# Reciprocals' transfers moved from SyncE to POOL, and weight pieces decoded three steps after their load

## The chip, the cores and the metric

The kernel runs on one core of one Trainium2 chip. Its engines are TensorE (PE, with its weight loads PEld), VectorE (DVE), ScalarE (ACT), GpSimd (POOL) and SyncE (SP), which here issues nearly all transfers. The metric is device time in microseconds (us), as a median of runs. Single rows come from one profiled execution.

## The reference, cut to what matters

Softcapped attention without a mask, a gated block that mixes over the sequence, and a block with a gated convolution, all in float32, one after the other.

```python
def _attn_ref(q, k, v, cap):                  # (2, 12, 448, 64)
    scores = scale * np.matmul(q, k.transpose(0, 1, 3, 2))
    scores = cap * np.tanh(scores / cap)
    scores = scores - np.max(scores, axis=-1, keepdims=True)
    attn = np.exp(scores)
    attn = attn / (np.sum(attn, axis=-1, keepdims=True) + 1e-09)
    return np.matmul(attn, v)

def _moe_ref(x, w_in, g_ln, w_sg, b_sg, w_out):   # x (2, 448, 768), w_in (768, 1024)
    h = gelu(x @ w_in)
    u, v = h[..., :512], h[..., 512:]
    v_n = layernorm(v) * g_ln
    v_s = np.einsum('ts,bsd->btd', w_sg, v_n) + b_sg[None, :, None]
    return x + (u * v_s) @ w_out

def _moe2_ref(x, w_in, conv_w, w_out):
    h = relu(x @ w_in)
    return (h * sigmoid(conv3(h, conv_w))) @ w_out
```

## The kernel before, in words

Every float32 product is made of three matmuls on numbers split into a high and a low part. The weights come from memory as 64-bit numbers and are decoded on the chip: `decode` loads a piece of 128 x 512 (512 KB, line 123) into a buffer named `f64` and turns it in three steps into the two parts. Step one is `L128` (ScalarE) and `L133` (VectorE), step two `L138`, `L141` and the cast `L147`, step three the subtraction `L150` (VectorE). `wait` says how many ticks after the load each step is issued, `bufs` how many pieces may be held at once.

Attention runs over 12 passes N, one pair of heads each, in two halves; a half is one round R, with two ticks in it (`tick()`), and `later(k, fn)` puts work k ticks ahead. In a half TensorE makes the scores `sc` (keys by queries), ScalarE takes tanh (`L312`) and exp (`L313`) of them into `raw`, and one round later, from round 13 on two rounds later, TensorE multiplies by the values (`pv`) and adds up the rows (`su`). VectorE sums two parts of `raw` beforehand (`sm`, `L333`), splits the keys and queries of a later pass (`L90`, `L93`, `L258`, `L259`) and copies the row sums out of `su` (`se<-su`, `L380`). There is one buffer for `su`, so the next pass's `su` waits for that copy, and one for `sc`, so the next scores wait for the tanh. In some rounds TensorE also starts the input product of the next block (`mo`, "fill").

The first ten passes are normalised in twos. I call such two passes a couple; there are five. When the second pass of a couple is summed, `norm` sends the sums from 4 to 128 partitions (`ss<-se`, line 385). Three ticks later `s1` adds a guard and takes the reciprocal (`L393`, `L394`) and writes it to memory (`d<-ss`, 397). `s1b` reads it back four times, spread over the partitions (`rb<-d`, 403), and `s2` multiplies (`E<-E,rb`, `L410`) and splits the result into `X`, the input of the next block (`L92` on ScalarE, `L93` on VectorE). The last two passes are normalised by TensorE.

```python
            later(3, s1)
            later(5, s1b)
            later(10, s2)
```

Each engine works in order. The order itself comes from a scheduler that issues instructions when its own model finds them ready, so ticks give the order of the program text and the scheduler may move an instruction within it. Line 442 is where pieces of `w_in` are asked for, in the rounds that `WIN` gives: 0, 3, 6, 8, 10, 12, 12, 16, 17, 19, 20 and 20.

Of the kernel before, what the change touches and what calls it, by code (L numbers as in the profile page):

```python
# [20 lines left out]
NK = DM // P  # L21
# [25 lines left out]
def stages(  # L47
# [17 lines left out]
    nc = tc.nc  # L65
    V, A, T, G = nc.vector, nc.scalar, nc.tensor, nc.gpsimd
# [4 lines left out]
    def pin(last):  # L71
        return tc.issue_after(last[0].ins) if last[0] is not None else ExitStack()
# [3 lines left out]
    def later(k, fn):  # L76
        due.setdefault(now[0] + k, []).append(fn)
# [7 lines left out]
    def f(ap):  # L85
        return ap.bitcast(F32)

    def split(raw, hi, lo, hi_eng="v"):
        if hi_eng == "v":
            V.tensor_copy(hi, raw)  # L90
        else:
            A.activation(hi, raw, AF.Copy)  # L92
        return V.tensor_tensor(out=lo, in0=raw, in1=f(hi), op=ALU.subtract)  # L93
# [17 lines left out]
    cw = const.tile([P, 2, 3 * NF], F32R, name="cw")  # L111
# [7 lines left out]
    def decode(hi, lo, src, pool, bufs, wait=(1, 2, 3), hi_eng="a", cols=512, low_eng="v"):  # L119

        n = src.shape[1]
        r = pool.tile([P, cols, 2], U32, tag="f64", name="f64", bufs=bufs)[:, :n]
        nc.sync.dma_start(r, src)
        h, l = r[:, :, 1], r[:, :, 0]

        def s1():
            with pin(lasta), pin(lastv):
                A.activation(f(h), f(h), AF.Copy, scale=2.0**-112)  # L128
                if low_eng == "a":

                    A.activation(l, l, AF.Copy, scale=0.93 * 2.0**-29)  # L131
                else:
                    V.tensor_scalar(  # L133
                        out=l, in0=l, scalar1=29, scalar2=None, op0=ALU.logical_shift_right
                    )

        def s2():
            V.scalar_tensor_tensor(  # L138
                out=l, in0=h, scalar=3, in1=l, op0=ALU.logical_shift_left, op1=ALU.bitwise_or
            )  # L140
            V.scalar_tensor_tensor(  # L141
                out=l, in0=h, scalar=0x80000000, in1=l, op0=ALU.bitwise_and, op1=ALU.bitwise_or
            )
            if hi_eng == "a":
                A.activation(hi, f(l), AF.Copy)
            else:
                V.tensor_copy(hi, f(l))  # L147

        def s3():
            V.tensor_tensor(out=lo, in0=f(l), in1=f(hi), op=ALU.subtract)  # L150

        for k, fn in zip(wait, (s1, s2, s3)):
            later(k, fn)

    def wdec(dst, src, k, c0, c1, pool, bufs, **kw):
        c = slice(c0 % dst.shape[3], c0 % dst.shape[3] + c1 - c0)
        decode(dst[:, 0, k, c], dst[:, 1, k, c], src[k * P : (k + 1) * P, c0:c1], pool, bufs, **kw)

    def wi_piece(src, h, k):
        return WI[h], src, k, h * DH, (h + 1) * DH  # L160
# [51 lines left out]

    def columns(pool):
        nc.sync.dma_start(gbc, g_ln.partition_broadcast(P))
        decode(cw[:, 0], cw[:, 1], conv_w, pool, 3)

    def attention(att, psa):

# [45 lines left out]
        def prep_k(n):  # L264
            _, kr = qraw.pop(n)
            K = Kt[n % 2]
            lastv[0] = split(kr, K[:, 0], K[:, 1], "a" if n == 0 else "v")
# [67 lines left out]
        def values(N, half):  # L335
# [28 lines left out]
            if half:  # L364
                del acc[N]
                norm(N, ps, su)

        def norm(N, ps, su):
            b, p = divmod(N, NPAIR)
            if N >= B * NPAIR - NFAST:  # L370
                return norm_pe(N, ps, su)

            j = N % 2
            if j == 0:
                pairs[:] = (
                    att.tile([P, 2, S // 2], F32, tag="se", name="se", bufs=2),
                    att.tile([P, 2, S], F32, tag="E", name="E", bufs=3),
                )
            se, e = pairs
            V.tensor_copy(se[:, j], su)  # L380
            A.activation(e[:, j], ps, AF.Copy)
            if j == 0:
                return
            ss = att.tile([P, 14], F32, tag="ss", name="ss", bufs=2)
            nc.sync.dma_start(ss, se[::32])
            rb = att.tile([P, 2, S], F32, tag="rb", name="rb", bufs=2)

            ds = []


            def s1():
                with pin(lastv):
                    V.tensor_scalar(out=ss, in0=ss, scalar1=guard, scalar2=None, op0=ALU.add)  # L393
                V.reciprocal(out=ss, in_=ss)  # L394
                ds.append(dr.tile([2, 2, 2, S // 2], F32, tag="d", name="d"))
                d = ds[0]
                nc.sync.dma_start(d.rearrange("h f j (p c) -> (h f j p) c", c=14), ss)

            def s1b():
                (d,) = ds  # L400
                for h in range(2):
                    for i in range(2):
                        nc.sync.dma_start(  # L403
                            rb[h * D : (h + 1) * D, i].rearrange("p (f c) -> p f c", f=2),
                            d[h, :, i].partition_broadcast(D),
                        )

            def s2():
                with pin(lastv):
                    V.tensor_tensor(out=e, in0=e, in1=rb, op=ALU.mult)  # L410
                with pin(lasta):
                    lastv[0] = split(e, X[:, 0, p - 1 : p + 1, b], X[:, 1, p - 1 : p + 1, b], "a")

            later(3, s1)
            later(5, s1b)
            later(10, s2)

        def norm_pe(N, ps, su):

# [19 lines left out]
        for R in range(2 * NN + LAGS[1]):  # L439
            N, half = divmod(R, 2)  # L440
            if R == 1:
                columns(att)
            for j, at in enumerate(WIN):
                if int(at * 4 + 1) // 2 == R:
                    wdec(*wi_piece(w_in, j // NK, j % NK), att, 3, hi_eng="v")
            if R < 2 * NN:
                if half == 0 and N + 2 < NN:
                    load(N + 2)
                scores(N, half)
                if half == 0 and N + 1 < NN:  # L450
                    prep_q(N + 1)
                    prep_k(N + 1)
            if R in FILL:

                i, k0, k1 = FILL[R]
                if k0 == 0:
                    fill[i] = psm.tile([P, 512], F32, tag="mo", name="mo")[:, :S]
                for k in range(k0, k1):
                    mmw(fill[i], 0, i, k, ordered)
                if k1 == NK:  # L460
                    u_done(0, i, fill[i])
            tick()
            if R - done >= LAGS[R >= LAGS[2]]:
                values(*divmod(done, 2))
                done += 1
            if half and N + 1 < NN:
                load_v(N + 1)
            tick()
# [411 lines left out]
```

## Time and profile before

| | |
|---|---|
| Time, median of 3 runs | 354.4 us (354.24 to 354.47) |
| Profiled execution: its time, its span | 356.76 us, 354.9 us |
| TensorE matmul, weight loads: busy | 333.1 us (94%), 252.5 us (71%) |
| VectorE, ScalarE, POOL: busy | 253.2 us (71%), 225.4 us (64%), 14.1 us (4%) |
| Mean granted clock of TensorE | 0.965 |
| Chain that ended last, by engine | PE 76%, DMA 10%, DVE 7%, SP's queue 3%, ACT 2% |

The span is the time from the first to the last instruction. Busy is the time in which the engine has an instruction in work; transfers are issued on a queue, which doesn't count as busy. Attention ends at about 141 us. POOL works in the first 5 us and then not before 141 us.

### The profile page before, as it was taken

The page shows a single profiled execution, that of the slowest core. Times are in us where ns is not written, and L with a number is a line of the kernel's source. Part 1 is how long each engine was busy: PE and PEld are TensorE (multiplying, and loading weights), DVE is VectorE, ACT ScalarE, POOL GpSimd, SP SyncE. Part 2 cuts the span into 40 slices and gives each one's busy share as a digit, 9 for nine tenths or more (in the row PEclk, how much of TensorE's full clock was granted, in tenths as well). Part 3 has the DMA queues.
Part 4 walks back from the last instruction along what each step waited for, and adds up shares of the span by engine and source line. Part 5 has one row for each costly group of instructions (what it writes and reads, how often), then busy time and mean ns, then how long its engine had stood idle before and what let it go on. Part 6 is the DMA issues. An engine that isn't in the chain of part 4 may idle for free.

```text
span 354.9 us, 5109 instructions
## 1 busy us (share of the span) xinstructions
PE 333.1 (94%) x1812; PEld 252.5 (71%) x1812; DVE 253.2 (71%) x491; ACT 225.4 (64%) x362; POOL 14.1 (4%) x37
## 2 busy tenths in 40 slices
PE   5699999796989989999999999999999999999992
PEld 4334454433445656889889999999999999999992
DVE  4367588694769536799799878999795999980000
ACT  2848889884798712757585546464785789872110
POOL 3000000000000000311011100000000000000000
PEclk9589999987899999999999999999999999999997
DMA  3865454637171011421323349000167022012211
GB/s 114 253 189 193 116 173 101 199 105 222 45 193 40 27 54 26 144 88 44 91 82 98 120 136 320 4 0 0 63 205 268 10 82 88 3 52 105 79 53 33
DMA packets 21518, 37.42 MB, mean 105 GB/s; under 512 B 4968, under 2 KB 12652, under 8 KB 21484
## 3 DMA queue, kind: packets, MB, share of 16 engines
q1 hardware_dynamic: 21452, 37.01, 33.7%
q8 instruction: 16, 0.26, 0.3%
q14 instruction: 18, 0.15, 0.1%
q0 software_dynamic: 32, 0.00, 0.0%
HBM read 34.18 MB, written 2.79 MB: 104 GB/s over the span
## 4 chain that ended last, share of the span: by engine, by line
PE 76%; DMA 10%; DVE 7%; SPq 3%; ACT 2%; issue 1%; DVEq 0%; ACTq 0%
PE mo L96 17%; PE mo L97 17%; PE mo L98 17%; PE pv L300 6%; PE sc L300 4%; DMA f<-in_w_in_dram 3%; PE mo L300 3%; PE mo L585 3%; PE su L300 3%; PE mo L587 3%; PE mo L586 3%; DMA ss<-se 2%; SPq L403 1%; DMA d<-ss 1%; DMA rb<-d 1%
## 5 line engine op out<-in xcount | busy, mean ns | idle before, releaser
L300 PE MATMUL sc<-Q,K 64*128 64x448 f32 (+1 forms) x252 | 41.8, 411 | 7.2 <-ACT raw L312 5.5
L300 PE MATMUL pv<-raw,V 128*64 128x448 f32 (+1 forms) x168 | 46.8, 601 | 0.4 <-ACT raw L313 0.4
L96 PE MATMUL mo<-X,WI 128*128 128x448 f32 x126 | 46.1, 367 | 0.0
L97 PE MATMUL mo<-X,WI 128*128 128x448 f32 x126 | 46.0, 366 | 0.0
L98 PE MATMUL mo<-X,WI 128*128 128x448 f32 x126 | 45.9, 365 | 0.0
L300 PEld LDWEIGHTS sc<-Q,K 64*128 64x128 f32 (+1 forms) x252 | 25.9, 197 | 22.9 <-ACT raw L312 8.4
L312 ACT ACTIVATE raw<-sc 128x1792 f32<-128x1792 f32 (+1 forms) x22 | 32.4, 1474 | 13.3 <-PE sc L300 11.9
L313 ACT ACTIVATE raw<-raw,one 128x1792 f32<-128x1792 f32 (+3 forms) x26 | 39.1, 1503 | 0.6
L128 ACT ACTIVATE f<-f 128x512 f32<-128x512 f32 (+3 forms) x57 | 30.9, 544 | 11.8 <-DMA f<-in_w_in_dram 6.8
L138 DVE SCALAR_TENSOR_TENSOR f<-f 128x512 uint32<-128x512 uint32 (+3 forms) x57 | 30.6, 547 | 9.2 <-ACT f L131 8.7
L97 PE MATMUL mo<-HG,W 128*128 128x448 f32 x96 | 34.7, 365 | 0.0
L98 PE MATMUL mo<-HG,W 128*128 128x448 f32 x96 | 34.7, 365 | 0.0
L96 PE MATMUL mo<-HG,W 128*128 128x448 f32 x96 | 34.1, 365 | 0.0
L141 DVE SCALAR_TENSOR_TENSOR f<-f 128x512 uint32<-128x512 uint32 (+3 forms) x57 | 30.7, 546 | 0.2
L300 PEld LDWEIGHTS pv<-raw,V 128*64 128x64 f32 (+1 forms) x168 | 12.3, 151 | 23.5 <-issue 20.6
L96 PEld LDWEIGHTS mo<-X,WI 128*128 128x128 f32 x126 | 23.6, 187 | 2.4 <-DVE u L177 0.4
L98 PEld LDWEIGHTS mo<-X,WI 128*128 128x128 f32 x126 | 23.6, 188 | 2.0
L97 PEld LDWEIGHTS mo<-X,WI 128*128 128x128 f32 x126 | 23.6, 188 | 2.0
L765 ACT ACTIVATE o<-mo 128x448 f32<-128x448 f32 x12 | 6.3, 543 | 26.1 <-PE mo L98 23.0
L131 ACT ACTIVATE f<-f 128x256 uint32<-128x256 uint32 (+2 forms) x44 | 22.6, 514 | 0.0
L97 PEld LDWEIGHTS mo<-HG,W 128*128 128x128 f32 x96 | 18.0, 188 | 1.4
L96 PEld LDWEIGHTS mo<-HG,W 128*128 128x128 f32 x96 | 18.0, 188 | 1.4
(137 smaller groups left out, 628.8 us busy)
## 6 DMA issues: line engine op xcount, KB each, us to landing
f<-in_w_in_dram SPq DMA_DIRECT2D x24, 512.0 KB, 4.7
f<-in_w_out_dram SPq DMA_DIRECT2D x24, 256.0 KB, 4.0
V<-in_vL_dram SPq DMA_DIRECT2D x12, 256.0 KB, 3.3
f<-in_w_out_dram SPq DMA_DIRECT2D x8, 384.0 KB, 3.3
qr<-in_qT_dram SPq DMA_DIRECT2D x24, 112.0 KB, 2.9
out_dram<-o SPq DMA_DIRECT2D x12, 224.0 KB, 1.9
rb<-d SPq DMA_DIRECT2D x20, 112.0 KB, 3.3
kr<-in_kT_dram SPq DMA_DIRECT2D x12, 112.0 KB, 2.5
```

The source lines that it names most:

```text
L96: matmul(ps, lhsT=whi, rhs=xhi, start=start, stop=False)
L97: matmul(ps, lhsT=whi, rhs=xlo, start=False, stop=False)
L98: matmul(ps, lhsT=wlo, rhs=xhi, start=False, stop=stop)
L128: A.activation(f(h), f(h), AF.Copy, scale=2.0**-112)
L131: A.activation(l, l, AF.Copy, scale=0.93 * 2.0**-29)
L138: V.scalar_tensor_tensor(out=l, in0=h, scalar=3, in1=l, op0=ALU.logical_shift_left, op1=ALU.bitwise_or)
L141: V.scalar_tensor_tensor(out=l, in0=h, scalar=0x80000000, in1=l, op0=ALU.bitwise_and, op1=ALU.bitwise_or)
L300: lastm[0] = T.matmul(*args, **kw)
L312: A.activation(raw[:, t], ps[:, t, :S], AF.Tanh, **sc)
L313: lasta[0] = A.activation(raw[:, t], raw[:, t], AF.Exp, scale=capc)
L585: T.matmul(ps, lhsT=xs(0, k), rhs=WI[1][:, 0, k], start=k == 0, stop=False)
L586: T.matmul(ps, lhsT=xs(0, k), rhs=WI[1][:, 1, k], start=False, stop=False)
```

## The change

Three edits. The transfers `ss<-se`, `d<-ss` and the four `rb<-d` of a couple are issued by POOL instead of SP. The step `s1b` follows one tick after `s1` instead of two, and the product `s2` eleven ticks after the sums instead of ten. The pieces of `w_in` during attention are decoded 3, 4 and 5 ticks after their load instead of 1, 2 and 3, with four buffers instead of three (the buffers are shared with `conv_w`, hence the 4 in `columns`).

```diff
     def columns(pool):
         nc.sync.dma_start(gbc, g_ln.partition_broadcast(P))
-        decode(cw[:, 0], cw[:, 1], conv_w, pool, 3)
+        decode(cw[:, 0], cw[:, 1], conv_w, pool, 4 if bounded else 3)
...
             ss = att.tile([P, 14], F32, tag="ss", name="ss", bufs=2)
-            nc.sync.dma_start(ss, se[::32])
+            G.dma_start(ss, se[::32])
...
-                nc.sync.dma_start(d.rearrange("h f j (p c) -> (h f j p) c", c=14), ss)
+                G.dma_start(d.rearrange("h f j (p c) -> (h f j p) c", c=14), ss)
...
-                        nc.sync.dma_start(
+                        G.dma_start(
                             rb[h * D : (h + 1) * D, i].rearrange("p (f c) -> p f c", f=2),
                             d[h, :, i].partition_broadcast(D),
                         )
...
             later(3, s1)
-            later(5, s1b)
-            later(10, s2)
+            later(4, s1b)
+            later(11, s2)
...
-                    wdec(*wi_piece(w_in, j // NK, j % NK), att, 3, hi_eng="v")
+                    wdec(*wi_piece(w_in, j // NK, j % NK), att, 4, hi_eng="v", wait=(3, 4, 5))
```

The scheduler makes a new order of it on SP, VectorE, ScalarE and POOL; TensorE's order stays the same. On POOL stand 30 issues, for each couple `ss`, `d` and four `rb`, where nothing stood. Three places follow. Numbers tell buffers of one name apart; they are counted anew in each program, so the same buffer can have two numbers.

First, SP's queue around the second piece of pass 6, which is `f64_630` before. `d_576` and `rb_508` belong to couple two, `V_625` holds the values of pass 6.

```order
L397 DMA d_576<-ss_506 128x14
L236 DMA qr_632<-in_qT_dram 64x448
L239 DMA kr0_89<-in_kT_dram 64x64
L403 DMA rb_508<-d_576 64x2x224 x4
L246 DMA V_625<-in_vL_dram 128x512
L123 DMA f64_630<-in_w_in_dram 128x1024
```

In the changed kernel the same piece is `f64_626`; `V_532` holds the values of pass 5.

```order
L237 DMA kr1_90<-in_kT_dram 64x448
L238 DMA kr1_90<-in_kT_dram 64x384
L236 DMA qr_538<-in_qT_dram 64x448 x2
L239 DMA kr1_90<-in_kT_dram 64x64
L246 DMA V_532<-in_vL_dram 128x512
L123 DMA f64_626<-in_w_in_dram 128x1024
```

The piece now stands one pass earlier, and the transfers of the couple are gone from ahead of it.

Second, VectorE before, around the product of couple three (`E_590`). `se_785<-su_748` copies the row sums of pass 6, `sm_736` and `sm_815` are the sums of passes 7 and 8, `f64_628` and `f64_630` the two pieces of pass 6.

```order
L147 CAST WI0_76<-f64_628 128x512
L147 CAST WI1_77<-f64_630 128x512
L150 TENSOR_TENSOR WI0_76<-f64_628,WI0_76 128x512
L150 TENSOR_TENSOR WI1_77<-f64_630,WI1_77 128x512
L333 TENSOR_TENSOR sm_736<-raw_721 128x896
L90 CAST K1_88<-kr1_90 128x512
L258 TENSOR_SCALAR Q_817<-qr_714,one_72 128x448
L93 TENSOR_TENSOR K1_88<-kr1_90,K1_88 128x512
L133 TENSOR_SCALAR f64_791<-f64_791 128x512
L259 SCALAR_TENSOR_TENSOR Q_817<-qr_714,one_72,Q_817 128x448
L410 TENSOR_TENSOR E_590<-E_590,rb_676 128x896
L380 COPY se_785<-su_748 128x224
```

In the changed kernel the end of the same stretch, up to the copy of pass 6 (now `se_785<-su_746`), reads as follows; `sm_725` is the sum of pass 7, and `E_424` belongs to couple two.

```order
L147 CAST WI1_77<-f64_626 128x512
L150 TENSOR_TENSOR WI0_76<-f64_624,WI0_76 128x512
L333 TENSOR_TENSOR sm_725<-raw_710 128x896
L90 CAST K1_88<-kr1_90 128x512
L150 TENSOR_TENSOR WI1_77<-f64_626,WI1_77 128x512
L258 TENSOR_SCALAR Q_817<-qr_703,one_72 128x448
L93 TENSOR_TENSOR X_75<-E_424,X_75 128x2x448
L393 TENSOR_SCALAR ss_673<-ss_673,one_72 128x14
L93 TENSOR_TENSOR K1_88<-kr1_90,K1_88 128x512
L133 TENSOR_SCALAR f64_791<-f64_791 128x512
L380 COPY se_785<-su_746 128x224
```

The product of couple three is gone from ahead of this copy, and the split of couple two's result and the guard of couple three have come in.

Third, VectorE in the changed kernel right behind that copy, down to the product of couple three, which is `E_589` here. `se_785<-su_823` copies the sums of pass 7, `sm_815` is the sum of pass 8.

```order
L259 SCALAR_TENSOR_TENSOR Q_817<-qr_703,one_72,Q_817 128x448
L394 RECIPROCAL ss_673<-ss_673 128x14
L333 TENSOR_TENSOR sm_815<-raw_800 128x896
L90 CAST K0_87<-kr0_89 128x512
L258 TENSOR_SCALAR Q_897<-qr_793,one_72 128x448
L93 TENSOR_TENSOR K0_87<-kr0_89,K0_87 128x512
L259 SCALAR_TENSOR_TENSOR Q_897<-qr_793,one_72,Q_897 128x448
L138 SCALAR_TENSOR_TENSOR f64_791<-f64_791 128x512
L380 COPY se_785<-su_823 128x224
L141 SCALAR_TENSOR_TENSOR f64_791<-f64_791 128x512
L410 TENSOR_TENSOR E_589<-E_589,rb_675 128x896
```

The product now follows the copy of pass 7 instead of standing ahead of the copy of pass 6.

## Rows read from the trace of the kernel before

**Rows 1.** Busy time of each engine by stretch, clock, transfers (all engines).

```profile
core 0: us, PE busy (x) PEld busy (x) DVE busy (x) ACT busy (x) POOL busy (x), PEclk, DMA share, GB/s
...
70.00:80.00 10.00, 10.00 (x67) 4.33 (x65) 9.90 (x20) 8.10 (x7) 0.00 (x0) 0.83 0.40 116
80.00:90.00 10.00, 6.79 (x34) 3.71 (x31) 4.67 (x9) 4.87 (x4) 0.00 (x0) 0.72 0.66 209
...
141.00:355.00 214.00, 207.44 (x1006) 188.44 (x1004) 160.03 (x316) 127.86 (x269) 10.93 (x15) 0.99 0.28 90
```

**Rows 2.** TensorE's waits from 18 to 142 us: total, times, longest.

```profile
PE su L300 <- DVE se L380: 4.2, 2, 3.2
PE sc L300 <- ACT raw L312: 2.2, 1, 2.2
```

**Rows 3.** Timeline of TensorE: start, us, operation, count, [idle before <- releaser].

```profile
26.19 1.34 PE L300 MATMUL pv<-raw,V 128*64 128x448 f32 x5 [0.43 <-ACT raw L313]
...
65.84 1.38 PE L300 MATMUL mo<-X,WI 128*128 128x448 f32 x6
69.37 1.49 PE L300 MATMUL sc<-Q,K 64*128 64x448 f32 x12 [2.15 <-ACT raw L312]
70.79 3.26 PE L300 MATMUL pv<-raw,V 128*64 128x448 f32 x8
...
80.36 1.72 PE L300 MATMUL pv<-raw,V 128*64 128x448 f32 x8
85.30 0.97 PE L300 MATMUL su<-sm,ones 128*32 128x224 f32 x8 [3.21 <-DVE se L380]
86.20 2.90 PE L300 MATMUL sc<-Q,K 64*128 64x448 f32 x9
88.91 2.44 PE L300 MATMUL mo<-X,WI 128*128 128x448 f32 x6
...
97.61 1.69 PE L300 MATMUL sc<-Q,K 64*128 64x448 f32 x9
...
106.08 0.58 PE L300 MATMUL su<-sm,ones 128*32 128x224 f32 x8 [0.96 <-DVE se L380]
```

**Rows 4.** Timeline of VectorE around the reciprocals, products and sums copies.

```profile
38.20 0.23 DVE L394 RECIPROCAL ss<-ss 128x14 f32<-128x14 f32 x1
...
45.49 1.09 DVE L410 TENSOR_TENSOR E<-E,rb 128x896 f32<-128x896 f32 x1 [0.21 <-DMA rb<-d]
...
58.03 1.08 DVE L333 TENSOR_TENSOR sm<-raw 128x896 f32<-128x896 f32 x1
...
74.75 0.26 DVE L394 RECIPROCAL ss<-ss 128x14 f32<-128x14 f32 x1
...
83.86 1.09 DVE L410 TENSOR_TENSOR E<-E,rb 128x896 f32<-128x896 f32 x1 [2.80 <-DMA rb<-d]
84.86 0.38 DVE L380 COPY se<-su 128x224 f32<-128x224 f32 x1
...
105.30 0.43 DVE L133 TENSOR_SCALAR f<-f 128x512 uint32<-128x512 uint32 x1 [2.69 <-DMA f<-in_w_in_dram]
```

**Rows 5.** Timeline from 56 to 70 us of SP's queue and of ScalarE.

```profile
57.87 2.57 SPq L403 DMA_DIRECT2D rb<-d  x4
...
61.18 1.53 SPq L123 DMA_DIRECT2D f<-in_w_in_dram  x1
...
67.47 0.68 ACT L128 ACTIVATE f<-f 128x512 f32<-128x512 f32 x1 [1.15 <-DMA f<-in_w_in_dram]
```

**Rows 6.** POOL's one transfer: its timeline row, and issue (KB, us to landing).

```profile
1.38 0.70 POOL L269 DMA_DIRECT2D one<-in_cap_dram  x1
...
one<-in_cap_dram POOLq DMA_DIRECT2D x1, 0.5 KB, 3.2
```

**Rows 7.** VectorE from 26 to 124 us by form: count, busy us, mean ns.

```profile
L333 DVE TENSOR_TENSOR sm<-raw 128x896 f32<-128x896 f32 x11 | 12.0, 1090 | 5.1 <-ACT raw L313 5.1
L150 DVE TENSOR_TENSOR WI<-f,WI 128x512 fp32r<-128x512 f32 x11 | 7.4, 695 | 0.2
...
L133 DVE TENSOR_SCALAR f<-f 128x512 uint32<-128x512 uint32 x10 | 4.3, 428 | 3.3 <-DMA f<-in_w_in_dram 3.3
```

## The prediction

> **What bounds the kernel now.** I first read the busy times by stretch, for the stages. From 141 us on TensorE computes for 207.44 of 214.00 us [rows 1], in the same order before and after, so the change can only shift that part. What can change is the time at which attention (0 to 141 us) ends.
>
> The waits of TensorE in that stage come next. Two entries carry most: VectorE's copy of the row sums (`se<-su`, 4.2 us in two waits) and the scores waiting for ScalarE's tanh (2.2 us) [rows 2]. The TensorE timeline gives place and price [rows 3]: 2.15 us idle before 69.37, 3.21 before 85.30 and 0.96 before 106.08. After the first two the clock falls: eight `pv` take 3.26 instead of 1.72 us; nine `sc` take 2.90 instead of 1.69, six `mo` 2.44 instead of 1.38, eight `su` 0.97 instead of 0.58. The granted clock of that second stretch is 0.72 of full [rows 1]. After the 0.96 us wait the `su` has its full speed.
>
> Then I followed who made the copy and the tanh late [rows 4, 5]. At 67.47 ScalarE waits 1.15 us for a piece of `w_in`, whose load SP issued at 61.18, behind four `rb` transfers; the tanh that TensorE needs stands behind it. At 83.86 VectorE starts the product with the reciprocals (`E<-E,rb`) after 2.80 us of waiting for `rb`, and the sums copy stands behind it, at 84.86. At 105.30 VectorE has waited 2.69 us for another piece of `w_in`, again ahead of a sums copy. So all three TensorE stalls are transfers that land after an in-order engine has come to them.
>
> **What goes.** If all three waits vanish, TensorE gains 2.15 + 3.21 + 0.96 = 6.32 us of idle time, and (3.26 - 1.72) + (2.90 - 1.69) + (2.44 - 1.38) + (0.97 - 0.58) = 4.20 us of low clock: **10.5 us**. For the pieces of `w_in` I expect just that. The second piece of pass 6 (`f64_630`) moves in SP's queue from behind four `rb` and the V of pass 6 to behind the V of pass 5, a pass earlier, and a piece's first step comes two ticks later; only the last piece is issued late (behind the buffer of `f64_791`). SP loses 30 issues, and no load waits behind one any more.
>
> **What the 30 issues cost on POOL.** POOL is idle there [rows 1]. Its only transfer in the trace occupied it for 0.70 us and landed 3.2 us after its issue [rows 6]. The SP issues of `rb` take 2.57 / 4 = 0.64 us [rows 5]. As POOL does nothing else between 5 and 141 us, 30 x 0.70 = 21 us is covered; what can cost time is only the latency from a reciprocal to its `rb`: one `d` and four `rb`, one after the other. On SP this took 7.06 us in the first couple (from 38.20 + 0.23 to 45.49) and 8.85 us in the third couple (from 74.75 + 0.26 to 83.86) [rows 4]. With five issues at 0.70 for 0.64 it is 7.4 to 9.15 us; I take the middle, **8.3 us**. No row shows a POOL issue beside a busy VectorE, and all of these are: the lower bound is 0.70 us, the upper one 0.70 plus one VectorE copy of 0.43 [rows 7], so 1.13 us. That would make the chain 10.45 us. I take 0.70, the only measured one.
>
> The Trainium skill speaks against this move: "SBUF — State Buffer", section "SBUF: two separate sides", says that descriptors of a POOL-issued transfer cannot be written while VectorE runs a copy in a two-port mode, and gives 620 ns alone against 3,100 ns beside such a copy. By its ratio an issue would take five times as long, 3.5 us as an estimate, and the chain would be about 22 us, so slower than before by far more than the change can win. The one POOL row agrees with the figure for the transfer alone; none here shows the other. It is part of the slow rival below.
>
> **Where the later product stands.** In the new order the third product follows the sums copy of pass 7, not that of pass 6, so the 3.21 us stall cannot come back in its old place. But the second product moves too: it now stands in a run of 38 VectorE instructions between the sum of pass 5 (`sm`, at 58.03) and the sums copy of pass 6. I count by that engine's prices [rows 7]: 6 long ones (three `sm`, two `X`, one product) at 1.09 make 6.5; 14 at 0.69 make 9.7; 15 at 0.43 make 6.4; three small ones at 0.23 [rows 4] make 0.7. Together 23.3 us. Each starts some 0.09 us before the one ahead ends (83.86 + 1.09 against 84.86 [rows 4]), so 37 x 0.09 = 3.3 goes off: 20.0 us. The copy is then done at 58.0 + 20.0 = 78.0 if nothing waits. TensorE without its stall comes to the `su` that needs it at 65.84 + 1.38 = 67.2, plus the stretch from 69.37 to 82.08 (80.36 + 1.72) less 1.54 of low clock, 11.2: 78.4 [rows 3]. So there are 0.4 us to spare.
>
> Inside the run the reciprocal of couple two ends after 11 instructions (6.2 us by the same prices, less 10 x 0.09), at 63.3, and the product is reached after 11 more (7.0 less 1.0 us), at 69.3. That leaves 6.0 us for a chain of 8.3: the product waits **2.3 us**, and TensorE, after the slack of 0.4, **1.9 us** (1.0 to 2.75 for chains of 7.4 and 9.15). This is the new stall. A stall of 2.15 us cost 1.54 us of clock afterwards and one of 0.96 us none; at 1.9 I take **1.5** (0 to 2.66, the loss after the 3.21 us stall).
>
> In the third couple the copy ahead of the reciprocal is done at 78.0 + 2.3 = 80.3, the reciprocal 0.8 us later, at 81.1. TensorE then does 0.6 us of `su`, 1.7 of `sc`, 1.4 of fill [rows 3], six `pv` and sixteen `su` (put at 1.7 and 1.1 from the eight of each): the sums of pass 7 are there at 86.8, and the product is reached after their copy and one decode step, at 87.7. That leaves 6.6 us for the chain of 8.3; the product waits 1.7. From it to the next copy VectorE has 14 instructions (7.3 us by the same prices), so that copy ends near 97, while TensorE wants it after the same eight groups as in the 11.2 us above, at 98.0: no stall, were it not for the late piece of `w_in` in between. This is issued when `f64_791` is done, about 2 us after the product starts, near 91.3, and reached near 96; loads take 6.2 us at worst (61.18 to 67.4 [rows 5]), so the copy may be a microsecond late. I put **0.5 us** (0 to 1.0). The first, fourth and fifth products have 8 us or more between reciprocal and product.
>
> **The sum.** 10.5 - 1.9 - 1.5 - 0.5 = 6.6 us. Other moved steps I put at nothing: at the start `pv` waits 0.43 us for ScalarE [rows 3], the most that the decode's move there can give back; the steps of `conv_w` stay where they are; the later decode still ends a pass or more before TensorE reads that piece. The profiled execution (356.76, its span 354.9) would come to 350.2. It lies 2.4 us above the median of the runs, 354.4, so the median comes to **347.8 us**. With the bounds above this case spans 10.5 - 1.0 = 9.5 us of gain to 10.5 - 2.75 - 2.66 - 1.0 = 4.1 us: 344.9 to 350.3.
>
> **Rivals.**
> 1. *Everything hides.* The chain on POOL, where nothing stands between its issues, fits into the 6.4 us that couple two has with its slack, and the gain is 9.5 to 10.5 us: 344. For it: nothing else uses POOL then. Against: the first couple took 7.06 us, with VectorE waiting at its end too.
> 2. *Some of it comes back.* POOL issues take 0.9 to 1.15 us beside VectorE; the chain is 9.3 to 10.6 us. Couple two then stalls TensorE for 2.9 to 4.2 us and costs 2.66 of clock, couple three 0.7 to 2.0 with up to 1.0 of clock: 6.3 to 9.8 of the 10.5 come back, a gain of 0.7 to 4.2 us, 350.2 to 353.7.
> 3. *Slower: VectorE holds up POOL's issues.* The place is the same, the wait of `E<-E,rb` ahead of a sums copy. With a chain C, TensorE stalls C - 6.4 in couple two and C - 9.1 + 0.5 in couple three. With clock losses of 2.66 and 1.0 this equals 10.5 at C = 10.9, an issue of 1.2 us instead of 0.70: from there on the change loses. If each issue waits behind two copies (0.70 + 2 x 0.43 = 1.56 us, C = 12.6), the stalls are 6.2 and 4.0 with 5.3 of clock: 5.0 us slower, 359. For it: in those stretches VectorE has hardly a gap. Against: its copies are short.
> 4. *The change does nothing*: what it takes away and what it brings cancel within 0.2% (0.7 us), about what a measurement of this kernel can tell from no change. That is issues of 1.15 to 1.25 us.
>
> Chances: the forecast 0.54, rival 1 0.06, rival 2 0.17, rival 3 0.16, rival 4 0.07. So faster by over 0.2% 0.77, same 0.07, slower 0.16. The range reaches from rival 1 to the end of rival 2, 344.0 to 353.5; outside are rival 3, rival 4 and the ends of rivals 1 and 2.
>
> **What the profile after would show.** Right: SP's issues of `ss`, `d` and `rb` stand on POOL at about 0.7 us each; VectorE's `L133` and ScalarE's `L128` no longer wait for `w_in` around 67 and 103 us; the third sums copy is not behind a product; one stall of about 2 us is left near 78 us, with VectorE waiting for `rb` just before. The last matmul of attention ends about 6 to 7 us earlier, and the rest has its old length. Wrong: POOL issues above 1 us or `rb` landing more than 9 us after its reciprocal, or longer VectorE instructions while POOL issues, which the count of 20.0 us leaves out; then the stalls at the sums copies are back. It is also wrong if another engine, ScalarE say, becomes the late one.

## The result, and the profile after

The changed kernel takes 351.49 us (median of 12 executions, 349.8 to 353.57) where the kernel before, run beside it, takes 354.41 (12 executions, 353.65 to 357.39): the ratio is 0.9915 with an interval of 0.9887 to 0.9942, so 2.9 us or 0.85% faster. That is inside the forecast's whole range (344.0 to 353.5) and a gain, as forecast, but less than half of the 6.6 us, and outside the 344.9 to 350.3 us that its main case spanned.

The profiled execution of the changed kernel took 349.80 us (span 347.9). Against the execution that the forecast was worked out from (356.76) it is 6.96 us shorter, close to the sum of 6.6. So either the sum is right and the usual execution differs from the profiled one, or it came out right by chance. That question runs through what follows.

Busy time by stretch in the changed kernel, for [rows 1]:

```profile
70.00:80.00 10.00, 7.99 (x59) 3.41 (x51) 7.96 (x14) 9.45 (x8) 0.00 (x0) 1.00 0.51 122
80.00:90.00 10.00, 9.05 (x65) 4.70 (x65) 6.20 (x13) 5.53 (x6) 3.68 (x6) 1.00 0.60 180
134.00:348.00 214.00, 207.61 (x1006) 188.55 (x1005) 160.15 (x316) 128.14 (x269) 10.91 (x15) 1.00 0.28 90
```

The last 214 us are as they were (207.61 busy for 207.44); attention ends 7 us earlier. In this execution the clock never falls behind a stall: 1.00 in both stretches, where it was 0.83 and 0.72. TensorE's waits, for [rows 2], here from 18 to 135 us:

```profile
PE su L300 <- DVE se L380: 3.2, 2, 2.5
...
PE sc L300 <- ACT raw L312: 0.6, 2, 0.5
```

The wait for the tanh fell from 2.2 to 0.6 us, that for the sums copy from 4.2 to 3.2. TensorE's timeline, for [rows 3], and VectorE's around the products, for [rows 4]:

```profile
66.75 1.49 PE L300 MATMUL sc<-Q,K 64*128 64x448 f32 x12 [0.17 <-ACT raw L312]
68.18 1.72 PE L300 MATMUL pv<-raw,V 128*64 128x448 f32 x8
...
80.95 0.59 PE L300 MATMUL su<-sm,ones 128*32 128x224 f32 x8 [2.47 <-DVE se L380]
81.47 1.69 PE L300 MATMUL sc<-Q,K 64*128 64x448 f32 x9
...
98.89 0.59 PE L300 MATMUL su<-sm,ones 128*32 128x224 f32 x8 [0.74 <-DVE se L380]
```

```profile
62.26 0.22 DVE L394 RECIPROCAL ss<-ss 128x14 f32<-128x14 f32 x1
...
72.03 1.09 DVE L410 TENSOR_TENSOR E<-E,rb 128x896 f32<-128x896 f32 x1 [2.59 <-DMA rb<-d]
...
80.52 0.38 DVE L380 COPY se<-su 128x224 f32<-128x224 f32 x1
81.41 0.23 DVE L394 RECIPROCAL ss<-ss 128x14 f32<-128x14 f32 x1
...
90.97 1.09 DVE L410 TENSOR_TENSOR E<-E,rb 128x896 f32<-128x896 f32 x1 [2.79 <-DMA rb<-d]
```

This is the stall that the forecast described: the product of couple two waits 2.59 us for `rb` (forecast 2.3), the sums copy of pass 6 comes 8.5 us after it, and TensorE stands 2.47 us (forecast 1.9). From the reciprocal's end to the product 9.55 us pass (62.48 to 72.03) and 9.33 us in couple three, where the forecast took 8.3.

POOL's issues of couple two and ScalarE's decode of the two pieces of pass 6, for [rows 6] and [rows 5]:

```profile
62.77 0.57 POOL L397 DMA_DIRECT2D d<-ss  x1 [13.43 <-DVE ss L394]
65.47 2.40 POOL L403 DMA_DIRECT2D rb<-d  x4 [2.13 <-DMA d<-ss]
67.85 0.75 POOL L385 DMA_DIRECT2D ss<-se  x1
```

```profile
68.06 1.24 ACT L128 ACTIVATE f<-f 128x512 f32<-128x512 f32 x2
```

An issue on POOL takes 0.57 to 0.75 us, though VectorE is busy for 8.73 of the 10 us from 60 to 70. ScalarE's two steps no longer wait for a piece, and they stand behind the tanh. Past the first 12 us no wait for `w_in` is left on VectorE or ScalarE in attention; at 11.38 us VectorE still waits 1.22 us for one (1.39 before).

### The profile page after: what moved, and what is told of

Same layout as the page of the kernel before. It is cut to its first block, busy times and chain, and to the rows that moved or that the text cites. A ratio compares the mean times of both kernels' runs of the same rounds, so it can differ in the third digit from the quotient of the medians.

```text
span 347.9 us, 5121 instructions
## 1 busy us (share of the span) xinstructions
PE 328.6 (94%) x1812; PEld 250.5 (72%) x1812; DVE 252.9 (73%) x491; ACT 225.5 (65%) x362; POOL 32.7 (9%) x67
## 5 line engine op out<-in xcount | busy, mean ns | idle before, releaser
L300 PE MATMUL sc<-Q,K 64*128 64x448 f32 (+1 forms) x252 | 40.5, 403 | 5.9 <-ACT raw L312 4.0
L300 PE MATMUL pv<-raw,V 128*64 128x448 f32 (+1 forms) x168 | 45.1, 579 | 0.0
L300 PEld LDWEIGHTS sc<-Q,K 64*128 64x128 f32 (+1 forms) x252 | 25.2, 193 | 20.9 <-ACT raw L312 8.1
L138 DVE SCALAR_TENSOR_TENSOR f<-f 128x512 uint32<-128x512 uint32 (+3 forms) x57 | 30.7, 548 | 10.8 <-ACT f L131 8.2
L97 PEld LDWEIGHTS mo<-X,WI 128*128 128x128 f32 x126 | 23.7, 188 | 2.0
```

The lines of the kernel that those rows point to most:

```text
L97: matmul(ps, lhsT=whi, rhs=xlo, start=False, stop=False)
L138: V.scalar_tensor_tensor(out=l, in0=h, scalar=3, in1=l, op0=ALU.logical_shift_left, op1=ALU.bitwise_or)
L300: lastm[0] = T.matmul(*args, **kw)
```

## Experiments

### Is the profiled execution the usual one?

Seven more executions with a trace, of the two kernels unchanged; the third of them was also timed against the kernel before.

> The kernel before, unchanged, for a second trace. Theory E (the profiled execution of before, 356.76, lost 4.2 us of clock behind two stalls that its usual execution, 354.4, loses only in part, so the sum counted as a gain what the median never had): the three stalls stand at the same places with 2.2, 3.2 and 1.0 us within half a microsecond, but less than 4.2 us of low clock behind them; 353.5 to 355.5. Rival F (the stalls themselves vary, because transfers land earlier or later): the idle times differ by a microsecond or more and explain the difference to 354.9.

> The same once more. Theory E: the time differs from the first trace of before by what its low clock behind the stalls differs, and by nothing else above half a microsecond. Rival F: by its idle times.

> The changed kernel, unchanged, for a second trace and on the chip of the other runs. Theory E: the same stalls as in its first trace, 2.5 us and 0.7 us, and a time of 350 to 352; the 1.7 us between the first profiled execution and the median are clock behind the 2.5 us stall. Rival G (the usual execution of the changed kernel has longer waits for rb than the profiled one, since all its transfers share the same engines): the stall in couple two is 3.5 us or more.

> The kernel before, one more execution. Theory S (the profiled execution that the sum was made from had a second stretch of low clock that is not usual): the first two stalls together are 5.3 to 5.8 us again, the first under 2 us with eight pv in 1.7 us after it, low clock only after the second; 354 to 355.7 us. Rival T (it is usual): first stall over 2 us, pv of 3.2 us after it, 356.5 us or more.

> The kernel before, another execution, with the same expectations: by theory S 354 to 355.7 us with one stretch of low clock in attention, by T 356.5 us or more with two.

> The changed kernel, one more execution. Theory S: one stall of 2.2 to 2.8 us before the su behind couple two's product; where the clock falls after it (eight su 0.97 us), 351.5 to 352.5 us; where it doesn't (0.59 us), 349.5 to 351 us. Rival T: other stalls over 1 us than that one.

> The changed kernel, another execution, with the same expectations.

TensorE's order is the same in both kernels, so the same instruction can be followed from trace to trace. The columns are the starts of five groups of eight `su` (the sixth, seventh, eighth, ninth and eleventh such group; the eighth is the one behind the second stall), the first matmul behind attention (`mo<-WI,X`), and the time of the execution, all in us.

| execution | a | b | c | d | f | g | time |
|---|---|---|---|---|---|---|---|
| before, profiled | 59.64 | 73.98 | 85.30 | 97.10 | 115.26 | 140.68 | 356.76 |
| before_again | 60.05 | 72.23 | 84.64 | 96.58 | 114.31 | 139.72 | 355.46 |
| before_again2 | 60.45 | 72.01 | 84.80 | 96.52 | 114.06 | 139.48 | 355.24 |
| before_look3 | 60.61 | 73.14 | 85.78 | 97.88 | 118.45 | 143.88 | 359.70 |
| before_look4 | 60.21 | 71.91 | 84.84 | 95.54 | 113.17 | 138.58 | 354.19 |
| after, profiled | 59.00 | 69.83 | 80.95 | 90.12 | 108.06 | 133.81 | 349.80 |
| after_again | 60.06 | 70.90 | 82.52 | 93.20 | 110.32 | 136.07 | 352.26 |
| after_look3 | 60.01 | 70.85 | 81.53 | 92.23 | 109.35 | 135.09 | 351.19 |
| after_look4 | 58.94 | 69.78 | 81.45 | 90.60 | 108.88 | 134.63 | 350.64 |

The stretch from a to b holds the first stall. It takes 14.34 us in the execution that the forecast used, but 11.56 to 12.53 in the other four, against 10.83 to 10.84 in all four of the changed kernel. In that stretch, removing the stall is worth 0.7 to 1.7 us, not the 3.51 us of that one pair. before_look4 shows why; its TensorE, and its ScalarE:

```profile
68.83 1.49 PE L300 MATMUL sc<-Q,K 64*128 64x448 f32 x12 [1.03 <-ACT raw L312]
70.25 1.72 PE L300 MATMUL pv<-raw,V 128*64 128x448 f32 x8
...
84.84 0.59 PE L300 MATMUL su<-sm,ones 128*32 128x224 f32 x8 [4.67 <-DVE se L380]
85.36 2.87 PE L300 MATMUL sc<-Q,K 64*128 64x448 f32 x9
```

```profile
66.23 1.38 ACT L128 ACTIVATE f<-f 128x512 f32<-128x512 f32 x2
```

Here the piece has landed in time, and TensorE stalls 1.03 us all the same, since two decode steps of 0.7 us stand ahead of the tanh. Lateness of the piece comes on top of that and changes from one execution to the next (1.15 us in [rows 5], none here). Only where it made the stall 2.15 us did the `pv` run at the lower clock behind it (3.26 us); after 1.52, 0.89, 1.87 and 1.03 us the eight `pv` take 1.72 us.

What a shorter first stall saves is in large part given back at the second, which grows as the first shrinks (3.21 after 2.15, 4.67 after 1.03): its end hangs on the `rb` of couple three, whose reciprocal starts at 74.59 to 75.79 us in all five traces of before, whatever the first stall was. From a to c the five take 24.35 to 25.66 us, the four of the changed kernel 21.52 to 22.51.

For before_again and before_again2 theory E holds in half. The single stalls differ from the first trace by up to 1.3 us (1.52, 4.13 and 0.54 us, and 0.89, 4.53 and 0.37), which it had denied; but they add up to 6.19 and 5.79 us, for 6.32 in the first, and what is gone from the time (1.30 and 1.52 us) is about the 1.54 us of low clock behind the first stall. The expectation of before_look3 missed on time and on sum (359.70 us, 1.87 + 4.36 = 6.23): there the third stall is 1.85 us as well, and the clock falls behind it too.

In the changed kernel the stall at c is there each time (2.47, 2.46, 2.12 and 2.44 us). The clock falls behind it in two of four executions, in after_again at once and in after_look3 one group later (eight `su` in 0.59 us, then nine `sc` in 2.52), which neither branch of the latter's expectation had. after_again, TensorE:

```profile
82.52 0.97 PE L300 MATMUL su<-sm,ones 128*32 128x224 f32 x8 [2.46 <-DVE se L380]
83.41 2.82 PE L300 MATMUL sc<-Q,K 64*128 64x448 f32 x9
```

From c to d it then takes 10.68 and 10.70 us, against 9.17 and 9.15 without: 1.5 us, the forecast's figure, in half of the executions. Timed once more against the kernel before, after_again gave 351.26 us (349.79 to 352.26, 6 executions) and a ratio of 0.9883 (0.9838 to 0.9928), about 4 us. Over all runs told here, the 56 executions of before have a median of 355.4 us (352.6 to 359.7) and the 20 of the changed kernel 351.4 (349.8 to 353.6), 4.0 us apart. That pool mixes measurements in which the kernel before had medians of 354.4 to 355.9, two of them without the changed kernel; so the usual gain is put at 3 to 4 us, and the runs below are best compared by their ratios.

### Which part of the change brings the gain?

Four kernels, each a part of the change; each ratio is to the kernel before, run beside it. The first keeps the pieces as they were and moves only the reciprocals' transfers, with their spacing:

```diff
-decode(cw[:, 0], cw[:, 1], conv_w, pool, 4 if bounded else 3)
+decode(cw[:, 0], cw[:, 1], conv_w, pool, 3)
...
-wdec(*wi_piece(w_in, j // NK, j % NK), att, 4, hi_eng="v", wait=(3, 4, 5))
+wdec(*wi_piece(w_in, j // NK, j % NK), att, 3, hi_eng="v")
```

> The transfers of the couples move to POOL with the new steps (4 and 11); the pieces of w_in keep the three buffers and the steps 1, 2 and 3. Theory A (the gain is the sum of the three TensorE stalls that go, less the new one in couple two; each part takes away the stalls that it touches): the product of couple three leaves its place ahead of the sums copy, so the 3.2 us stall goes, but the two waits for w_in (2.15 and 0.96 us) stay or move; 352.5 to 354. Theory B (all of the gain comes from the earlier pieces; POOL only moves the wait): no gain, 354.4 or more.

It takes 351.31 us (ratio 0.9905, 0.9874 to 0.9936): the gain of the whole change without the earlier pieces, better than either theory had it. Past 20 us no engine waits for a piece of `w_in`; the first stall is 0.88 us, and the longest is behind the product of couple three, with low clock after it:

```profile
92.39 0.59 PE L300 MATMUL su<-sm,ones 128*32 128x224 f32 x8 [2.04 <-DVE se L380]
...
94.73 3.29 PE L300 MATMUL pv<-raw,V 128*64 128x448 f32 x6
```

The second does the pieces alone: SP issues `ss`, `d` and (not shown) the four `rb`, in the old spacing:

```diff
-G.dma_start(ss, se[::32])
+nc.sync.dma_start(ss, se[::32])
...
-G.dma_start(d.rearrange("h f j (p c) -> (h f j p) c", c=14), ss)
+nc.sync.dma_start(d.rearrange("h f j (p c) -> (h f j p) c", c=14), ss)
...
-later(4, s1b)
-later(11, s2)
+later(5, s1b)
+later(10, s2)
```

> The pieces of w_in with four buffers and steps 3, 4 and 5; the transfers of the couples stay on SP with steps 5 and 10. Theory A: no engine waits for w_in any more, but in this order the product of couple three still stands ahead of the sums copy of pass 6, and the product of couple two ahead of that of pass 5, so a stall of 3 us or more at a sums copy stays, behind a wait for rb; 352.5 to 354.5. Theory B: the whole gain, 351.5.

It takes 351.46 us (0.9916, 0.9876 to 0.9957), again the whole gain, by another way. Its TensorE:

```profile
52.27 0.58 PE L300 MATMUL su<-sm,ones 128*32 128x224 f32 x8 [1.40 <-DVE sm L333]
61.52 0.58 PE L300 MATMUL su<-sm,ones 128*32 128x224 f32 x8 [1.23 <-DVE sm L333]
...
74.25 1.69 PE L300 MATMUL sc<-Q,K 64*128 64x448 f32 x9 [1.31 <-ACT raw L312]
```

The stalls are in other places, none over 1.4 us, and the clock stays up behind them; the stall of 3 us that theory A expected at a sums copy is not there. The third is the changed kernel with SP as the issuing engine (`nc.sync` for `G` in its three places):

> The changed kernel with its steps and pieces, but the couples' transfers issued by SP: only the issuing engine differs from the changed kernel. The products and reciprocals stand on VectorE as in the changed kernel. Theory A: the chain from reciprocal to rb is the shortest on an idle queue (9.8 us on POOL in the profiled run, couple two), and on SP loads get in between, so the waits at the products of couples two and three are 0.5 to 2 us longer and loads are held up behind rb: 352 to 353.5. Rival C (the issuing engine does not matter, the steps do): as the changed kernel, 351.5.

It takes 350.89 us (0.9893, 0.9854 to 0.9932), no slower than the changed kernel. SP's queue, VectorE and TensorE:

```profile
66.53 2.57 SPq L403 DMA_DIRECT2D rb<-d  x4
```

```profile
63.27 0.23 DVE L394 RECIPROCAL ss<-ss 128x14 f32<-128x14 f32 x1
...
71.52 1.09 DVE L410 TENSOR_TENSOR E<-E,rb 128x896 f32<-128x896 f32 x1 [2.36 <-DMA rb<-d]
...
81.19 0.37 DVE L380 COPY se<-su 128x224 f32<-128x224 f32 x1
```

```profile
81.62 0.58 PE L300 MATMUL su<-sm,ones 128*32 128x224 f32 x8 [2.25 <-DVE se L380]
```

Issues, wait and stall are those of POOL within 0.25 us, but not by the same way. VectorE's order is not the one that the expectation took for granted: the product stands one decode step (`L138`) earlier and the sums copy one instruction later, so that 9.7 us lie between them instead of 8.5. And the product starts 8.02 us after the reciprocal's end (63.50 to 71.52) instead of 9.55. The two differences cancel; what the run shows is an equal time, not an equal chain. The Trainium skill says under "DMA: Bandwidth & Descriptors", section "Issuing engines are not separate DMA queues", that a second issuing engine saves only sequencer time; the time of this run agrees. The fourth is the kernel before with nothing changed but the two ticks:

```diff
-later(5, s1b)
-later(10, s2)
+later(4, s1b)
+later(11, s2)
```

> The kernel before with only the spacing of the steps changed (read-back four ticks after the sums, product eleven): SyncE still issues everything, the pieces of w_in are loaded and decoded as before. Theory E (what counts is only the place of the product on VectorE and of the piece's load on SyncE's queue): with this spacing the second piece of pass 6 is issued ahead of the four rb of couple two, so ScalarE no longer waits for it near 67 us, and the product of couple two stands behind the sums copy of pass 5: 350.5 to 352 us, as fast as the whole change; the product of couple two waits 2 to 3.5 us and one TensorE stall of 1 to 2.5 us is left at a sums copy. Theory P (POOL is needed, because on SyncE the five issues of a couple hold up the loads behind them): VectorE or ScalarE still waits over 1 us for a piece of w_in ahead of a sums copy or a tanh, and the time is 353 to 355 us.

It takes 352.27 us (351.19 to 353.36; 0.9895, 0.9858 to 0.9933), 0.3 us outside what theory E gave for its median, but below the 353 to 355 of P: no engine waits for a piece, although SP still issues everything, because the scheduler now puts the piece's load ahead of the four `rb`. The product of couple two, for which theory E gave a wait of 2 to 3.5 us, waits 0.56; it is that of couple three which waits. What is left, on VectorE and TensorE:

```profile
90.00 1.09 DVE L410 TENSOR_TENSOR E<-E,rb 128x896 f32<-128x896 f32 x1 [4.00 <-DMA rb<-d]
```

```profile
69.39 1.50 PE L300 MATMUL sc<-Q,K 64*128 64x448 f32 x12 [0.88 <-ACT raw L312]
...
92.66 0.59 PE L300 MATMUL su<-sm,ones 128*32 128x224 f32 x8 [2.36 <-DVE se L380]
```

So POOL brings no time of its own, with the new spacing and without the earlier pieces (pool_only against spacing_only) as with both (the changed kernel against sp_spaced); POOL with nothing else changed was not run. And the two other parts don't add up: each alone takes the stalls down to one or a few that cost about the same.

### Is the rest the product that waits for `rb`?

If so, a product that stands further from its reciprocal is faster. First one more tick, `later(12, s2)` for `later(11, s2)`:

> The changed kernel with the product twelve ticks after the sums instead of eleven. In the order that results, the reciprocal of couple two stands ahead of the sum of pass 5 instead of eleven instructions behind it, and the product keeps its place; couple three's reciprocal stands one pass earlier too. Theory A (what is left is the wait of the products for rb, 2.6 and 2.8 us on VectorE, 2.5 and 0.7 us on TensorE): both stalls go, 348 to 349.5, and the spread of the runs gets smaller. Rival D (the 1.7 us between the profiled execution of the changed kernel, 349.8, and its median 351.5 come from elsewhere, say from the start or from the clock): the gain is at most 1 us, 350.5 to 351.5, and the spread stays.

It takes 348.59 us (347.9 to 350.37; 0.9856, 0.9817 to 0.9894). The scheduler also moved couple two's reciprocal ahead. VectorE and TensorE:

```profile
67.67 1.08 DVE L410 TENSOR_TENSOR E<-E,rb 128x896 f32<-128x896 f32 x1
...
83.54 1.09 DVE L410 TENSOR_TENSOR E<-E,rb 128x896 f32<-128x896 f32 x1 [0.65 <-DMA rb<-d]
```

```profile
79.42 0.59 PE L300 MATMUL su<-sm,ones 128*32 128x224 f32 x8 [0.83 <-DVE se L380]
```

The product of couple two doesn't wait, 0.83 us of the 2.47 is left, and the clock stays up. The same spacing on SP:

> The changed kernel with SyncE as the issuing engine again and the product twelve ticks after the sums. Theory E (the engine that issues doesn't matter where the loads are three ticks ahead): 348 to 349.5 us, as the same spacing on POOL; the products wait under 1 us each, and no engine waits for a piece of w_in. Theory P: SyncE's issues hold up the loads of keys, queries or pieces, and the time is 350.5 us or more.

It takes 349.0 us (347.99 to 350.42; 0.98, 0.9765 to 0.9835), the same as on POOL.

Then the other direction: a longer chain, made by cutting each `rb` transfer in two, so that POOL issues eight.

```diff
-G.dma_start(rb[h * D : (h + 1) * D, i].rearrange("p (f c) -> p f c", f=2),
-            d[h, :, i].partition_broadcast(D))
+for f2 in range(2):
+    G.dma_start(rb[h * D : (h + 1) * D, i, f2 * (S // 2) : (f2 + 1) * (S // 2)],
+                d[h, f2, i].partition_broadcast(D))
```

> The changed kernel with each of the four rb transfers cut in two, so eight issues on POOL of half the size; VectorE's order is the same. Theory A (TensorE's new stall is the chain from reciprocal to rb less what VectorE has to do meanwhile): the chain gets 4 x 0.6 = 2.4 us longer, the product of couple two waits 5.0 instead of 2.6 us, TensorE 4.9 instead of 2.5, couple three adds about 2 us more than before: 353.5 to 357. Rival H (the wait is the transport of the bytes, not the issues): same time as the changed kernel within 0.7 us.

It takes 348.22 us (346.75 to 350.14; 0.9803, 0.9755 to 0.9852): 3 us faster than the changed kernel, where every theory had it slower or the same. POOL, VectorE and TensorE:

```profile
66.19 4.29 POOL L404 DMA_DIRECT2D rb<-d  x8 [2.12 <-DMA d<-ss]
```

```profile
74.95 1.09 DVE L411 TENSOR_TENSOR E<-E,rb 128x896 f32<-128x896 f32 x1 [1.11 <-DMA ss<-se]
...
79.74 0.39 DVE L380 COPY se<-su 128x224 f32<-128x224 f32 x1
```

```profile
80.18 0.58 PE L300 MATMUL su<-sm,ones 128*32 128x224 f32 x8 [1.07 <-DVE se L380]
```

The chain is longer, as meant: 63.20 to 74.95, 11.75 us. (The row names `ss<-se`, which POOL issues right behind the `rb`; the product doesn't read `ss`.) But the scheduler, which counts the longer chain in its model, put the product behind seven more decode instructions. So the wait falls to 1.11 us, and from the product to the copy it is 4.8 us instead of 8.5. The expectations had taken VectorE's order as fixed. Two kernels between these ends test that reading: with one `rb` cut (five issues) the product moves behind two more instructions, with two cut (six issues) behind four.

> The changed kernel with one of the four rb transfers cut in two, so five issues. The scheduler then puts the product of couple two two decode instructions later on VectorE. Theory E (the stall is the arrival of rb, plus what stands between product and sums copy): rb lands 0.5 us later, the product is reached 1.3 us later and waits 1.8 us (1.4 to 2.4, after some 2.6), and TensorE's stall before the su behind it is 1.65 us (1.2 to 2.1, after 2.5). Theory L (the longer chain alone counts): wait 3.1, stall 3.0 us. One execution, 350 to 351.5 us by E.

> The changed kernel with two of the four rb transfers cut in two, so six issues; the product of couple two stands four decode instructions later than in the changed kernel. Theory E: rb lands 1.1 us later, the product is reached 2.5 us later and waits 1.1 us (0.7 to 1.8); TensorE's stall before the su is 1.15 us (0.8 to 1.7), no low clock after it. Theory L: wait 3.7, stall 3.5 us. One execution, 348.5 to 350.5 us by E, 351 to 353 by L.

They took 349.91 and 348.39 us (one execution each). Wait and stall of couple two with four, five, six and eight issues are 2.59 and 2.47, 2.06 and 1.29, 0.46 and 0.30, 1.11 and 1.07 us. rb_in_six, VectorE and TensorE:

```profile
72.22 1.09 DVE L417 TENSOR_TENSOR E<-E,rb 128x896 f32<-128x896 f32 x1 [0.46 <-DMA rb<-d]
...
78.54 0.38 DVE L380 COPY se<-su 128x224 f32<-128x224 f32 x1
```

```profile
78.97 0.59 PE L300 MATMUL su<-sm,ones 128*32 128x224 f32 x8 [0.30 <-DVE se L380]
```

Theory L, by which the stall grows with the chain (3.0 and 3.5 us), falls. E has the direction and for five issues the size (expected 1.65 of stall, 1.2 to 2.1); with six it falls below its range (0.30 for 0.8 to 1.7), as `rb` landed no later than with four issues (9.55 us after the reciprocal in both). Both times lie 0.1 us below what E gave. product_12, sp_product_12 and rb_in_eight beat both kernels; in the single execution rb_in_six does too.

## Why the prediction was right in sign and wrong in size

**The step that failed** is the first term of *What goes*: 2.15 us for the first stall and, of the 4.20 us of low clock, the 1.54 us behind it, 3.69 in all, counted as what every execution loses, and carried to the median by a constant 2.4 us. By the table the stretch a to b gives 3.51 us in the profiled pair, but with the other four executions of before (mean 11.99 us against 10.84) only 1.15. That is 2.5 us less than counted, 1.54 of it clock that the others don't lose there; between the forecast's 6.6 and the usual 3 to 4 us lie 2.6 to 3.6. The execution profiled was the one of five in which the piece landed late enough to cost clock as well. Nor was all of that stall a late transfer, as *What bounds the kernel now* has it: 1.03 us of it is there when the piece is in time. And the first two stalls were added as if each went by itself. From a to c they make 3.69 + 1.31 = 5.00 us in the forecast; the profiled pair gave 3.71 there, and the other four executions of before 2.57.

That the profiled pair nonetheless comes near the sum, 6.87 us at g, is in part luck. Its six stretches gave 0.64, 3.51, 0.20, 2.63, 0.22 and -0.33 us, where 0, 3.69, 1.31, 1.16, 0.46 and 0 were forecast: at the second stall 1.1 us were missing, and behind it 1.5 us too much came in, as the clock didn't fall in that execution of the changed kernel.

All terms, as means over the traces of the table:

| stretch | forecast us | before, 5 traces | after, 4 traces | gain us |
|---|---|---|---|---|
| start to a | 0 | 60.19 | 59.50 | 0.69 |
| a to b: first stall and its clock | 2.15 + 1.54 = 3.69 | 12.46 | 10.84 | 1.62 |
| b to c: second stall | 3.21 - 1.9 = 1.31 | 12.42 | 11.27 | 1.15 |
| c to d: clock behind it | 2.66 - 1.5 = 1.16 | 11.65 | 9.93 | 1.72 |
| d to f: third stall | 0.96 - 0.5 = 0.46 | 18.33 | 17.62 | 0.71 |
| f to g: last two passes | 0 | 25.42 | 25.75 | -0.33 |

The gains add up to 5.6 us, and to 4.7 without before_look3, the slowest execution of all.

- *The new stall.* Place, cause and engine were right. It was mis-sized by only 0.2 to 0.6 us, as two errors nearly cancel: the chain takes 9.55 us (9.1 to 10.1 in the other traces) and not 8.3, and the product is reached 6.96 us after the reciprocal and not 6.0. So the sign of being wrong, `rb` more than 9 us after its reciprocal, came true, and the bound of 9.15 was too low. The issues were priced well (0.57 to 0.75 us); what was short are the landings: POOL waits 2.13 us for `d`, and the product starts 4.2 us after the last issue of `rb` ends (67.87 to 72.03). Where SP issues, in the kernel before as in sp_spaced, spacing_only and prefetch_only, the waiting products of couples two and three start 7.1 to 8.9 us after their reciprocals, in the four traces of the changed kernel and in pool_only 8.9 to 10.1. The long landings are those beside other traffic (last section). The count of VectorE's run held: from the `sm` at 57.20 to the copy's end at 80.90 are 23.7 us, less the waits of 2.59 and 0.61, 20.5 for a forecast of 20.0.
- *Low clock behind it.* The size was right (1.5 us), but it comes in two executions of four; this gave back some 0.7 us.
- *Third stall.* Right on average; without before_look3 the gain there is 0.15.
- *Nothing elsewhere.* The start gave more than the 0.43 us allowed: in three of the five executions of before a `sc` waits there as well, 0.23 to 0.93 us, which it didn't in the profiled one. Behind b an `sc` waits 0.47 or 0.48 us for the tanh in each trace of the changed kernel, where it waited 0.19 at most. The last two passes cost 0.33 us, as `rp` waits 1.00 us for VectorE instead of 0.60.
- *Rivals.* "Everything hides" is out, a stall of 2.1 to 2.5 us is in each trace. "Some of it comes back" gave 0.7 to 4.2 us of gain, which holds the result, but not by its cause: POOL's issues are not longer beside VectorE. "VectorE holds up POOL's issues" is refuted by the same rows, and by couple four, where the `rb` land in 3.0 us with VectorE busy for 6.26 of 6.37 us. The rule of the Trainium skill that stood behind it ("SBUF — State Buffer", section "SBUF: two separate sides") shows no effect on these transfers; whether VectorE's instructions beside them are of the mode that it means, the traces don't say.

What stays open is why the piece lands up to 1.2 us later in one execution than in another.

## What to carry to other kernels

A stall that is a late transfer has a size that changes with each execution: before its price goes into a sum against the median, it should be read in three or four traces, and split into what always stands ahead (here two decode steps) and what is lateness. Two stalls that follow each other share their time, so one that shrinks can lengthen the next: their worth is read over the stretch that holds both. Where three parts of a change all move instructions of one in-order engine, their gains are not to be added: two of them alone each gave all of it here. And an edit that lengthens a transfer chain can be faster, where a scheduler answers it by placing the consumer later; so the order comes first, then the durations.

## What the runs showed of the hardware

- How long the `rb` take to land goes here with how busy the transfer engines are, and not with VectorE. In the changed kernel, for the `rb` of couple two and then of couple four, the stretch from the first issue and the median time to landing read:

```profile
65.47:71.87 6.40, 5.75 (x41) 3.05 (x40) 3.37 (x6) 6.33 (x6) 3.13 (x5) 1.00 0.97 245
rb<-d POOLq DMA_DIRECT2D x4, 112.0 KB, 4.6
```

```profile
101.87:108.24 6.37, 6.37 (x49) 2.66 (x51) 6.26 (x11) 6.14 (x9) 3.12 (x5) 1.00 0.39 115
rb<-d POOLq DMA_DIRECT2D x4, 112.0 KB, 3.0
```

  With VectorE busy for 3.37 us and the transfer engines for 0.97 of the time the median is 4.6 us, with 6.26 us and 0.39 it is 3.0. In after, after_again and pool_only the five couples with a share of 0.85 to 0.97 take 4.5 to 5.5 us, the ten with 0.35 to 0.51 take 2.9 to 3.9. This is read from the traces; no run set the share by itself.

- The same wait leaves TensorE's clock at full speed or not: after 2.47 us (after, profiled) eight `su` take 0.59 us, the 2.4 GHz level, after 2.46 us (after_again) 0.97, the 1.2 GHz level. In before_look4 a wait of 4.67 us was followed by eight `su` in 0.59 and then nine `sc` in 2.87 us. What decides was not found.
- The mean granted clock doesn't rank executions. At the start the record and the durations disagree; windows and TensorE of after_look3, then of after_look4:

```profile
10.00:20.00 10.00, 7.79 (x27) 3.34 (x31) 3.35 (x8) 6.98 (x9) 0.00 (x0) 1.00 0.87 216
```

```profile
16.47 3.26 PE L300 MATMUL pv<-raw,V 128*64 128x448 f32 x8
```

```profile
10.00:20.00 10.00, 7.79 (x33) 3.41 (x35) 4.12 (x9) 6.83 (x9) 0.00 (x0) 0.56 0.92 236
```

```profile
16.32 2.97 PE L300 MATMUL pv<-raw,V 128*64 128x448 f32 x8
```

The first reads a clock of 1.00 over eight `pv` that take 3.26 us, the second 0.56 over eight that take 2.97; at full speed they take 1.72. TensorE is busy 7.79 us in both. So a mean of 0.989 (351.19 us) or 0.982 (350.64 us) says little of where time went, and the durations in the stretch say it.
